# A chain of linear attention and two expert layers: a new order for the first block, and fixed places for five weights of the second expert

## The chip, the cores and the metric

The kernel runs on one core of a Trainium2 chip. The metric is the device time of one execution in microseconds, the median of several runs. PE is the matmul engine (TensorE), DVE the vector engine, ACT the scalar engine, POOL is GpSimd, and SP is the engine whose queue issues nearly all transfers.

## What is computed

```python
def _attn_ref(r, k, v, w, u):            # B, H, S, D = 4, 8, 768, 48
    for t in range(S):
        kt, vt, rt, wt = (k[:, :, t], v[:, :, t], r[:, :, t], w[:, :, t])
        cur = np.einsum('bhd,bhe->bhde', u[None] * kt, vt)
        y[:, :, t] = np.einsum('bhd,bhde->bhe', rt, state + cur)
        state = wt[:, :, :, None] * state + np.einsum('bhd,bhe->bhde', kt, vt)
...
def _moe_ref(x, w1, w2, w3, w_out):      # 3072 tokens, 384 -> 1024 -> 1024 -> 384
    return ((x @ w1) * (x @ w2) @ w3) @ w_out
...
def _moe2_ref(x, w_in, w_out):           # 384 -> 2048 -> 384
    h = x @ w_in
    return (h - np.tanh(h)) @ w_out
```

The weights come as 64-bit floats, the rest as 32-bit floats.

## The kernel before

The 3072 tokens are 24 attention chunks of 128 (chunk 0 to 23) and six blocks of 512 (block 0 to 5); four chunks make the x of one block. Attention works chunk by chunk: DVE runs two scans over the decay (`running`, `backward`), `decayed` multiplies them into r and k, PE makes the scores (`psA`), the transposed keys (`psk`), the state's update (`psu`) and the outputs (`psy`); ACT copies scores out of PSUM, POOL masks them, and DVE or PE puts the term with u on the diagonal (`put_diag`, from chunk 4 on; `diag` before). `x_round` on ACT and `x_rest` on DVE split the result into a rounded value and a remainder, since every large product is made of three products of halves (`three`, lines 206 to 208). Six transfers on SP (`spread`, `xt<-y`) bring the last 16 dimensions of each head into place at the end of a block.

Each block of the first expert has eight parts f: `phase1` makes x·w1 and x·w2 of 128 columns (`psa`, `psb`, 18 products), the gate multiplies them (ACT copies a, DVE multiplies, ACT rounds and DVE takes the remainder of g), and `phase2` adds the part to the block's sums (`acc`, 9 products). w3 and w_out are folded into one matrix W on the chip, in eight folds (`fold`, `psW`, line 486), each of eight products in plain 32-bit.

Weights must be converted before use. `fetch` brings one of 64-bit words into one of three staging buffers (`st`); `scaled` and `tail` on ACT (lines 168 and 174) take its upper part and three more bits; `joined` on DVE (lines 178 and 180) puts them together in one of three buffers (`cm`) or in place; and for the split weights `rounded` on ACT (line 199) and `rest` on DVE or POOL (line 202) make the halves. w1/w2 come in 8 pieces of 768 columns, w_out in 4 of 768, w3 in 16 of 512, and the second expert's weights in 16 of 768 (`w45`).

The order of the work is set in three ways:

- For block 0, the first chunks and all weights of expert one, the list `ORDER` (line 43) names 409 steps one by one. `lwa3` fetches w1/w2 part 3, `waa3`, `wba3`, `wja3` are its scale, tail and join, `wha3` and `wsa3` its halves; `o` stands for w_out, `x` and `y` for the halves of w3. `F0`, `Fa0`, `Fd0` are fold 0 and its halves, `P0` is phase 1 of part 0, `Ga` to `Gs` its gate, `Q0` its phase 2, and `Sa2`, `O2`, `Y2` and the like are attention steps of chunk 2. Each engine gets its instructions in the order of the list.
- Blocks 1 to 4 are written by `pair` (line 779): a pair is one chunk of attention, two blocks ahead, and two parts f of the block, at i = 0 to 3. Its text is the order too.
- Block 5 of expert one (`moe1` with `hooks`) and the six blocks of expert two (`moe2`) are written plainly, and a scheduler orders them; it may put their instructions ahead into places of the pair loop.

Two weights of expert two are converted in the pair loop, in blocks 2 and 3: fetched at i = 1, scaled and joined at i = 2, split at i = 3. The other fourteen are converted by `conv2` from block 5 on. After each block `store` copies the three sums out and takes their largest absolute values, which, with those of the weights (`largest`), decide at the end whether a short series is good enough for the tanh.

Of the kernel before, what the change touches and what calls it, by code (L numbers as in the profile page):

```python
# [15 lines left out]
ALU = mybir.AluOpType  # L16
# [10 lines left out]
KT = DM // 128  # L27
# [13 lines left out]


ORDER = """
LP0 LK0 lwa3 lwa1 lwa2 Da0 LP1 Dr0 K0 Db0 LK1 Dk0 Sd0 Dc0 waa3 wba3 Sa0 Se0 wja3 waa1 Sf0 wba1 St0 lwy3 Sb0 wja1 Sk0
Sm0 SB0 Su0 waa2 SM0 Da1 lwa0 wha3 O0 T0 Dr1 wba2 U0 Db1 LP2 wha1 LK2 V0 Dk1 W0 wsa3 Sd1 X0 Dc1 way3 Se1 wby3 Sf1 Y0
Sa1 wsa1 St1 SB1 Da2 Sb1 SM1 Sk1 wja2 Sm1 waa0 Su1 Dr2 O1 T1 wba0 lwo0 Dk2 U1 Db2 wha2 LP3 Sd2 V1 LK3 wsa2 W1 Se2 Dc2
Sf2 X1 wao0 Y1 Sa2 wja0 St2 Sb2 SB2 Sm2 Da3 lwo1 Sk2 SM2 wbo0 Su2 Dk3 Dr3 wha0 O2 T2 Db3 U2 LP4 wsa0 Sd3 V2 LK4 Dc3
wao1 W2 Se3 X2 wjo0 Sa3 Sf3 SB3 Da4 lwo2 Sb3 St3 SM3 wbo1 Y2 Sm3 Sk3 wjy3 Dr4 O3 Db4 lwo3 wao2 wjo1 Dc4 Su3 LK5 LN4 V3
wbo2 W3 T3 X3 lwa4 wjo2 wao3 U3 Sa4 LP5 wbo3 Y3 lwy0 P0 Sb4 wjo3 SB4 Sm4 Dt4 lwx0 SM4 waa4 De4 St4 LN5 P1 C4 Ga0 Sk4
wba4 Da5 way0 wby0 wja4 Dr5 O4 wax0 Ga1 Dt5 Db5 lwa5 wbx0 Su4 LK6 X4 P2 V4 wha4 T4 Dc5 Gm0 wsa4 Gb0 wjx0 waa5 U4 W4  # L50
lwx2 Sa5 LP6 wjy0 Ga2 wba5 P3 Gm2 lwy2 Sb5 wja5 Gb2 Sm5 SB5 wax2 SM5 Gs2 lwx3 wha5 Y4 wbx2 F0 Da6 Ga3 De5 Dr6 Gm3 LN6
Db6 Gb3 Gs3 Dc6 wsa5 P4 Fa0 Gm1 way2 Fd0 Gb1 Dt6 wjx2 wby2 wax3 Gs1 lwa6 wbx3 wjy2 Sa6 Ga4 P5 wjx3 lwy4 Sb6 SB6 Sm6
De6 lwx1 SM6 Gm4 LN7 waa6 C5 Gb4 F3 wba6 C6 Ga5 Gs4 Dt7 wja6 Gm5 wha6 lwx4 St6 Gs0 F2 Fa3 wsa6 wax1 Sk6 Fd3 wbx1 way4
wjx1 wby4 lwy1 wjy4 Su6 Fa2 O5 wax4 lwx5 Fd2 wbx4 wjx4 Q0 way1 LP7 LK7 V5 X5 T6 lwa7 W5 wby1 U6 Y5 F4 Gb5 wjy1 Gs5
lwx7 LP8 Da7 De7 Dr7 Db7 LN8 F1 Fa4 wax5 Fd4 Dc7 waa7 wbx5 wax7 wjx5 wba7 Da8 lwy6 wbx7 Sa7 Dt8 Fa1 wja7 O6 Sb7 SB7
St7 LK8 V6 Sm7 Fd1 X6 lwy7 Sk7 wjx7 Q1 SM7 way6 Dr8 W6 wha7 lwy5 C7 P6 wby6 wsa7 Y6 wjy6 way7 wby7 Q2 De8 lwx6 Ga6
wjy7 LN9 Su7 Gm6 F7 T7 Gb6 Db8 U7 LP9 Gs6 Dc8 O7 Fa7 way5 Fd7 wax6 Q3 LK9 wby5 X7 wjy5 wbx6 P7 V7 wjx6 W7 Y7 Z7 Q4 Ga7
Gm7 Gb7 F5 Gs7 F6 Fa5 Fd5 Q5 Fa6 Fd6 Q6 Q7
""".split()


# [30 lines left out]
def body(ctx: ExitStack, tc, rT, kT, wP, wS, vN, rN, kN, vT, uB, uN, uP, w12, w3F, wo, w45, out):  # L92
# [466 lines left out]

    def phase3(bp, xt, f, parts):  # L560
# [95 lines left out]
    def largest(f):
        nc.vector.tensor_reduce(
# [87 lines left out]
    with tc.manual_schedule():  # L745
# [17 lines left out]
    def conv2_halves(f):  # L763
        second.pop()
        w45t[f] = halves(early[f], f"w45_{f}", False)
# [10 lines left out]
        preps[n][k] = a1.tile([128, DM], F32, tag=tag, name=k)  # L776
        nc.sync.dma_start(preps[n][k], src[n])

    def pair(blk, i, acc, weights):
        n = (blk + 1) * per + i  # L780
        now = n < NCH
        nx = n + 1 < NCH
        nn = n + 2 < NCH
        out_ = (lambda e: x2d[blk, :, e, :], blk)
        done = lambda f, g: (step(g, lambda: Wt[f], f, NF, acc, out_), drain(LA1))
        f = 2 * i
        if now:
            scores(n)
            scores_out(n, 0)
            mask(n, 0)  # L790
            scores_out(n, 1)
            mask(n, 1)
            turn = n % NC < NC - 1
            if turn:
                turned(n)
                turned_out(n)
        pa, pb = phase1(xtile(blk), f)
        a = gate_a(pa)
        if nn:
# [92 lines left out]

    for blk in range(NB):
        extra = {f: [] for f in range(NF2)}
        if 0 < blk < NB - 1:
            for j in range(6):
                extra[2 * j + 2].append(lambda n=6 * blk - 6 + j: bounds(n))
        if blk == NB - 1:
            extra[2].append(decide)
        if blk == 0:  # L900
            for f in range(NF2):
                extra[f].append(conv2)
        if blk + 1 < NB:
            extra[8].append(lambda: nxt.append(load_x(x2d[blk + 1])))
        moe2(bp, nxt[blk], blk, extra, NF2 - 3 if blk == NB - 1 else NF2)
# [134 lines left out]
```

## Time and profile before

| | us |
|---|---|
| median of 3 runs | 907.2 (905.99 to 907.22) |
| the profiled execution | 908.82 |
| its span, first to last instruction | 907.1 |
| PE busy in the span | 861.9 |
| DVE, ACT, POOL busy | 614.3, 483.0, 227.3 |

The page is to be read stage by stage: block 0 with its weights up to 175 us, the pair loop to about 450, block 5 of expert one to about 510, and then expert two, which goes on to the end. PE takes its instructions strictly in order, so what stands behind a waiting product waits too.

### The profile page before, as it was taken

The numbers are of one execution on the slowest core, as the hardware profiler recorded it, in microseconds if no ns is written. First come the engines' busy times: TensorE is split into PE (matmuls) and PEld (weight loads), VectorE is DVE, ScalarE is ACT, GpSimd is POOL, SyncE is SP. The second block draws the span as 40 slices with busy tenths as digits, with TensorE's granted clock in tenths as the row PEclk, the third lists the DMA queues.
The fourth block names the chain that finished last, engine by engine and source line by source line (L and its number), as shares of the span: only waits on it lengthen the run. The fifth ranks groups of instructions, "written<-read, shape, count | busy, mean of one in ns | idle before, by whom it ended". The sixth has DMA issues, their size and how long they took to land.

```text
span 907.1 us, 12892 instructions
## 1 busy us (share of the span) xinstructions
PE 861.9 (95%) x4762; PEld 690.8 (76%) x4762; DVE 614.3 (68%) x884; ACT 483.0 (53%) x879; POOL 227.3 (25%) x223
## 2 busy tenths in 40 slices
PE   5879999999999999799999899999999999999996
PEld 4766767778777777577888688888888888888885
DVE  6889884365666666665567977667667577586763
ACT  4546652123223224422467766596696786786662
POOL 4356241053344543435226310010010010000000
PEclk9789999999999999899999999999999999999999
DMA  8586574134443364631253020220220310300001
GB/s 287 196 273 201 168 262 129 47 111 129 116 154 109 96 242 134 215 117 53 54 180 134 21 61 1 68 72 0 71 69 1 94 47 1 106 23 0 36 1 38
DMA packets 51623, 93.31 MB, mean 103 GB/s; under 512 B 5152, under 2 KB 22688, under 8 KB 51552
## 3 DMA queue, kind: packets, MB, share of 16 engines
q1 hardware_dynamic: 51552, 92.41, 32.2%
q8 instruction: 39, 0.64, 0.3%
q14 instruction: 32, 0.26, 0.1%
HBM read 80.99 MB, written 9.44 MB: 100 GB/s over the span
## 4 chain that ended last, share of the span: by engine, by line
PE 49%; issue 3%; POOL 2%; DVE 1%; DMA 1%; ACT 1%; SPq 0%; ACTq 0%; POOLq 0%
PE acc L206 8%; PE acc L208 8%; PE acc L207 8%; PE psh L206 7%; PE psh L208 7%; PE psh L207 7%; POOL w L202 1%; DMA st<-w 1%; PE psa L206 1%; PE psa L207 1%; PE psa L208 1%; PE psb L207 1%; PE psb L206 1%; PE psb L208 1%; PE psy L395 0%
## 5 line engine op out<-in xcount | busy, mean ns | idle before, releaser
L516 DVE TENSOR_TENSOR g<-psh,g 128x512 fp32r<-128x512 f32 (+1 forms) x99 | 66.4, 672 | 55.3 <-ACT g L515 55.0
L206 PE MATMUL psh<-xt,w 128*128 128x512 f32 x252 | 98.1, 389 | 0.5 <-DVE g L516 0.5
L208 PE MATMUL psh<-xt,w 128*128 128x512 f32 x252 | 98.0, 389 | 0.0
L207 PE MATMUL psh<-xt,w 128*128 128x512 f32 x252 | 98.0, 389 | 0.0
L206 PE MATMUL acc<-g,w 128*128 128x512 f32 x252 | 98.0, 389 | 0.0
L207 PE MATMUL acc<-g,w 128*128 128x512 f32 x252 | 98.0, 389 | 0.0
L208 PE MATMUL acc<-g,w 128*128 128x512 f32 x252 | 98.0, 389 | 0.0
L515 ACT CAST g<-psh 128x512 fp32r<-128x512 f32 (+1 forms) x99 | 56.3, 570 | 63.0 <-DVE psh L582 63.0
L512 POOL TENSOR_TENSOR xt<-x2l,xt 128x512 fp32r<-128x512 f32 x18 | 24.4, 1366 | 258.4 <-ACT xt L511 258.3
L580 DVE TENSOR_TENSOR psh<-psh,z 128x512 f32<-128x512 f32 (+1 forms) x99 | 67.2, 679 | 27.0 <-ACT z L577 26.7
L581 DVE SCALAR_TENSOR_TENSOR psh<-s,psh 128x512 f32<-128x512 f32 (+1 forms) x99 | 67.1, 678 | 19.0 <-ACT s L578 12.6
L577 ACT ACTIVATE z<-psh 128x512 f32<-128x512 f32 (+1 forms) x99 | 57.6, 582 | 30.9 <-PE psh L208 29.3
L582 DVE SCALAR_TENSOR_TENSOR psh<-s,psh 128x512 f32<-128x512 f32 (+1 forms) x99 | 67.2, 679 | 9.5
L578 ACT ACTIVATE s<-z,qa 128x512 f32<-128x512 f32 (+1 forms) x99 | 70.5, 712 | 2.4
L579 ACT ACTIVATE s<-z,qa 128x512 f32<-128x512 f32 (+1 forms) x99 | 69.0, 697 | 0.0
L515 ACT CAST g<-psb 128x512 fp32r<-128x512 f32 x40 | 23.4, 585 | 84.9 <-DVE psb L843 48.8
L206 PE MATMUL psa<-xt,w 128*128 128x512 f32 x144 | 61.8, 429 | 6.9 <-DMA xt<-y 3.3
L337 POOL TENSOR_SCALAR_AFFINE_SELECT A<-A 128x512 f32<-128x512 f32 x48 | 37.6, 804 | 90.9 <-ACT A L332 90.7
L206 PE MATMUL psb<-xt,w 128*128 128x512 f32 x144 | 56.9, 395 | 2.5 <-ACT a L531 2.2
L208 PE MATMUL acc<-g,W 128*128 128x512 f32 x144 | 56.3, 391 | 2.2 <-DVE W L202 2.2
L206 PE MATMUL acc<-g,W 128*128 128x512 f32 x144 | 57.8, 401 | 0.0
L207 PE MATMUL psa<-xt,w 128*128 128x512 f32 x144 | 57.6, 400 | 0.0
(141 smaller groups left out, 1984.0 us busy)
## 6 DMA issues: line engine op xcount, KB each, us to landing
st<-w SPq DMA_DIRECT2D x24, 768.0 KB, 4.4
st<-w3F SPq DMA_DIRECT2D x16, 512.0 KB, 4.7
P<-wP SPq DMA_DIRECT2D x24, 258.0 KB, 2.8
ws<-wS SPq DMA_DIRECT2D x24, 256.0 KB, 3.4
kd<-kT SPq DMA_DIRECT2D x24, 256.0 KB, 3.8
rd<-rT SPq DMA_DIRECT2D x24, 256.0 KB, 4.0
vn<-vN SPq DMA_DIRECT2D x24, 256.0 KB, 3.6
wb<-wP SPq DMA_DIRECT2D x24, 256.0 KB, 3.4
```

The lines of the kernel that those rows point to most:

```text
L206: nc.tensor.matmul(ps, lhs(0), rhs(1), start=start, stop=False)
L207: nc.tensor.matmul(ps, lhs(0), rhs(0), start=False, stop=False)
L208: nc.tensor.matmul(ps, lhs(1), rhs(0), start=False, stop=stop)
L337: nc.gpsimd.affine_select(out=A, in_=A, pattern=[[0, NP], [1, C]], compare_op=ALU.is_gt, fill=0.0, base=0, channel_multiplier=-1)
L515: nc.scalar.copy(t[:, 0, :], x)
L516: nc.vector.tensor_sub(t[:, 1, :], x, t[:, 0, :].bitcast(F32))
L577: nc.scalar.activation(out=z, in_=p, func=AF.Square)
L578: nc.scalar.activation(out=s1, in_=z, func=AF.Square, scale=QS, bias=qa[:, 0:1])
L579: nc.scalar.activation(out=s2, in_=z, func=AF.Square, scale=QS, bias=qa[:, 1:2])
L580: nc.vector.tensor_mul(p, p, z)
L581: nc.vector.scalar_tensor_tensor(out=p, in0=s1, scalar=QB1, in1=p, op0=ALU.add, op1=ALU.mult)
L582: nc.vector.scalar_tensor_tensor(out=p, in0=s2, scalar=QB2, in1=p, op0=ALU.add, op1=ALU.mult)
```

## The change

`ORDER` is replaced by another list of the same 409 steps, the first line of each is shown here. The rest of the diff:

```diff
 ORDER = """
-LP0 LK0 lwa3 lwa1 lwa2 Da0 LP1 Dr0 K0 Db0 LK1 Dk0 Sd0 Dc0 waa3 wba3 Sa0 Se0 wja3 waa1 Sf0 wba1 St0 lwy3 Sb0 wja1 Sk0
...
+LP0 LK0 lwo0 lwo1 lwx0 Da0 LP1 Dr0 K0 Db0 LK1 Dk0 Sd0 Dc0 wao0 wbo0 Sa0 Se0 wjo0 wao1 Sf0 wbo1 St0 wax0 wjo1 lwy0 Sb0
...
     def store(acc, dst, blk=None):
         for e in range(KT):
-            if blk is not None:
-                nc.vector.tensor_reduce(out=xm[:, e, blk : blk + 1], in_=acc[e], op=ALU.max, axis=AX.X, apply_absolute_value=True)
             o = ev.tile([128, TB], F32, tag="a", name="o")
...
             nc.sync.dma_start(dst(e), o)
+        for e in range(KT if blk is not None else 0):
+            nc.vector.tensor_reduce(out=xm[:, e, blk : blk + 1], in_=acc[e], op=ALU.max, axis=AX.X, apply_absolute_value=True)
...
     second = list(range(NF2))[::-1]
+    early = []
...
         f = second.pop()
-        w45t[f] = halves_of(w45[f], f"w45_{f}", False, not bound)
-        if bound:
-            largest(f)
+        if bound and f < len(early):
+            w45t[f] = halves(early[f], f"w45_{f}", False)
+        else:
+            w45t[f] = halves_of(w45[f], f"w45_{f}", False, not bound)
...
         split_ps(pb, g)
-        if weights and i == 3:
-            conv2_halves(blk - 2)
-            largest(blk - 2)
         if now and turn:
...
-        if weights and i == 1:
+        if i == 0 or (blk, i) == (NB - 2, 1):
             conv2_fetch()
...
         a = gate_a(pa)
+
+        w = blk - 1 if i == 1 else blk if (blk, i) == (NB - 2, 2) else None
+        if w is not None:
+            conv2_act(w)
+        if i == 2 and blk < 3:
+            conv2_halves(blk - 1)
         nc.vector.tensor_mul(pb, pb, a)
         g = gp.tile([128, 2, TB], F32R, tag="g", name="g")
         split_ps(pb, g)
-        if weights and i == 2:
-            conv2_act(blk - 2)
-            conv2_join(blk - 2)
+        if w is not None:
+            conv2_join(w)
         done(f, g)
...
     for blk in range(NB):
         extra = {f: [] for f in range(NF2)}
+        if blk == 1:
+            for f in range(NF2):
+                extra[f].append(lambda f=f: largest(f))
```

So five weights, 0 to 4, are fetched in the pair loop and joined at i = 1 of blocks 1 to 4 and at i = 2 of block 4; weights 0 and 1 are split at i = 2 of blocks 1 and 2, and weights 2 to 4 stay joined until block 5.

Three places of the built order. The first is on PE behind chunk 1, whose last row is the product with `y_148`. Before, chunk 2 follows at once:

```order
L414 MATMUL psy<-y_148 128x128 x3
L327 MATMUL psA<-rd,kd 128x128 x8
L349 MATMUL psk<-ident,kd 128x128 x4
L362 MATMUL psu<-vn,ks 64x48 x8
L389 MATMUL psy<-rd,Sb_117 64x128 x8
L395 MATMUL psy<-A,vn 64x128 x2
L401 MATMUL psy<-ident,vc 64x128 x2
```

and with the change:

```order
L414 MATMUL psy<-y_148 128x128 x3
L486 MATMUL psW<-wo,w_202 128x384 x4
L486 MATMUL psW<-wo,w_254 128x384 x4
L486 MATMUL psW<-wo,w_378 128x384 x4
L486 MATMUL psW<-wo,w_400 128x384 x4
L327 MATMUL psA<-rd,kd 128x128 x8
L486 MATMUL psW<-wo,w_452 128x384 x4
L486 MATMUL psW<-wo,w_444 128x384 x4
```

Folds 0 and 1 (two rows of `psW` each) now stand ahead of chunk 2's scores, and fold 2 behind them.

The second place is on DVE, in block 3, from the product of the gate at the end of the pair i = 2 to the sum that updates the state in i = 3. Before:

```order
L843 TENSOR_TENSOR psb<-psb,a 128x512
L516 TENSOR_TENSOR g<-psb,g 128x512
L178 SCALAR_TENSOR_TENSOR cm<-cm,cl 128x768
L180 SCALAR_TENSOR_TENSOR cm<-st,cm 128x768
L178 SCALAR_TENSOR_TENSOR cm<-cm,cl 128x768
L180 SCALAR_TENSOR_TENSOR cm<-st,cm 128x768
L343 COPY_PREDICATED A<-eye,cd 128x512 x2
L178 SCALAR_TENSOR_TENSOR cm<-cm,cl 128x768
L804 TENSOR_TENSOR psb<-psb,a 128x512
L180 SCALAR_TENSOR_TENSOR cm<-st,cm 128x768
L516 TENSOR_TENSOR g<-psb,g 128x512
L657 TENSOR_REDUCE wm<-w_1_3233 128x3
L370 TENSOR_TENSOR Sb_117<-psu,Sb_118 128x4x48
```

and with the change:

```order
L846 TENSOR_TENSOR psb<-psb,a 128x512
L516 TENSOR_TENSOR g<-psb,g 128x512
L343 COPY_PREDICATED A<-eye,cd 128x512 x2
L804 TENSOR_TENSOR psb<-psb,a 128x512
L516 TENSOR_TENSOR g<-psb,g 128x512
L370 TENSOR_TENSOR Sb_118<-psu,Sb_117 128x4x48
```

The joins of the early weight and of two that had been put ahead from block 5, and the weight's maximum, no longer stand there.

The third place is on POOL in block 2, from the products for the diagonal to the state's decay. Before:

```order
L280 TENSOR_TENSOR rn<-rn,un 128x384
L281 TENSOR_TENSOR rn<-rn,kn 128x384
L337 AFFINE_SELECT A<-A 128x512 x2
L202 TENSOR_TENSOR w_0_2614<-cm,w_0_2614 128x768
L375 TENSOR_TENSOR Sb_117<-Sb_117,P 128x4x48
```

and with the change (weight 1 in place of weight 0):

```order
L280 TENSOR_TENSOR rn<-rn,un 128x384
L281 TENSOR_TENSOR rn<-rn,kn 128x384
L202 TENSOR_TENSOR w_1_2557<-cm,w_1_2557 128x768
L337 AFFINE_SELECT A<-A 128x512 x2
L375 TENSOR_TENSOR Sb_117<-Sb_117,P 128x4x48
```

The subtraction that makes a weight's remainder stands ahead of the masks instead of behind them.

## Rows read from the trace of the kernel before

**Rows 1.** The page's first part: each engine's busy us, share, instructions.

```profile
PE 861.9 (95%) x4762; PEld 690.8 (76%) x4762; DVE 614.3 (68%) x884; ACT 483.0 (53%) x879; POOL 227.3 (25%) x223
```

**Rows 2.** PE's timeline, first block: start us, us, what, count [idle before <-releaser].

```profile
35.44 0.91 PE L414 MATMUL psy<-y 128*128 128x128 f32 x6
...
39.27 0.67 PE L362 MATMUL psu<-vn,ks 128*64 128x48 f32 x16 [1.11 <-ACT ks L354]
...
43.70 0.91 PE L414 MATMUL psy<-y 128*128 128x128 f32 x6
...
60.02 0.50 PE L206 MATMUL psa<-xt,w 128*128 128x512 f32 x1 [1.56 <-DVE xt L434]
...
77.37 1.16 PE L327 MATMUL psA<-rd,kd 48*128 48x128 f32 x16 [1.60 <-POOL kd L303]
...
84.27 5.32 PE L486 MATMUL psW<-wo,w 128*128 128x384 f32 x16
...
130.59 0.50 PE L208 MATMUL acc<-g,W 128*128 128x512 f32 x1 [2.21 <-DVE W L202]
...
175.10 0.39 PE L206 MATMUL psa<-xt,w 128*128 128x512 f32 x1
```

**Rows 3.** DVE's timeline, first block: chunk 2's backward pass begins; chunk 3's last remainder.

```profile
30.39 0.54 DVE L289 RECIPROCAL ends<-R 128x64 f32<-128x64 f32 x1
...
59.41 0.55 DVE L434 TENSOR_TENSOR xt<-psy,xt 128x384 fp32r<-128x384 f32 x1
```

**Rows 4.** Groups by shape, conversions on DVE, ACT: busy us, mean ns | idle.

```profile
L178 DVE SCALAR_TENSOR_TENSOR cm<-cm,cl 128x768 int32<-128x768 int32 x28 | 30.1, 1073 | 12.3 <-ACT cm L168 7.0 <-ACT cd L312 2.9 <-ACT cl L174 2.4
...
L180 DVE SCALAR_TENSOR_TENSOR cm<-st,cm 128x768 int32<-128x768 int32 x24 | 29.9, 1246 | 0.5
...
L180 DVE SCALAR_TENSOR_TENSOR wo<-st,cm 128x768 int32<-128x768 int32 x4 | 5.8, 1454 | 0.1
...
L178 DVE SCALAR_TENSOR_TENSOR cm<-cm,cl 128x512 int32<-128x512 int32 x16 | 12.8, 801 | 6.4 <-ACT cl L174 6.4
...
L180 DVE SCALAR_TENSOR_TENSOR w<-st,cm 128x512 int32<-128x512 int32 x16 | 12.3, 768 | 1.1
...
L202 DVE TENSOR_TENSOR w<-cm,w 128x768 fp32r<-128x768 f32 x8 | 8.7, 1086 | 0.0
...
L168 ACT ACTIVATE cm<-st 128x768 f32<-128x768 f32 x28 | 25.4, 909 | 15.3 <-DMA st<-w 8.4 <-POOL w L202 1.9 <-DVE w L202 1.6
...
L174 ACT ACTIVATE cl<-st,qa 128x768 int32<-128x768 uint8 x28 | 27.9, 996 | 11.5 <-DMA st<-w 9.7 <-DVE cm L178 1.9
```

**Rows 5.** PE's timeline: first rows of blocks 2, 3 and 4, and waits between.

```profile
238.44 0.47 PE L206 MATMUL psa<-xt,w 128*128 128x512 f32 x1
...
308.05 0.47 PE L206 MATMUL psa<-xt,w 128*128 128x512 f32 x1 [1.92 <-ACT A L332]
...
362.75 0.67 PE L362 MATMUL psu<-vn,ks 128*64 128x48 f32 x16 [1.43 <-ACT ks L354]
...
376.56 1.16 PE L327 MATMUL psA<-rd,kd 48*128 48x128 f32 x16 [2.48 <-POOL kd L303]
...
381.63 0.76 PE L206 MATMUL psa<-xt,w 128*128 128x512 f32 x1 [3.33 <-DMA xt<-y]
```

**Rows 6.** Windows, block 4's start: us, PE, PEld, DVE, ACT, POOL, PEclk, DMA.

```profile
380.00:390.00 10.00, 8.37 (x41) 6.57 (x42) 2.93 (x6) 1.51 (x3) 0.00 (x0) 0.72 0.49 140
```

**Rows 7.** DVE's timeline, block 2: the join of an early weight.

```profile
289.77 0.96 DVE L178 SCALAR_TENSOR_TENSOR cm<-cm,cl 128x768 int32<-128x768 int32 x1 [1.08 <-ACT cl L174]
```

**Rows 8.** ACT's and POOL's timelines, block 2's end: remainder's rounding; the masks, twice.

```profile
306.37 0.58 ACT L515 CAST g<-psb 128x512 fp32r<-128x512 f32 x1 [3.46 <-DVE psb L843]
...
290.28 2.25 POOL L337 TENSOR_SCALAR_AFFINE_SELECT A<-A 128x512 f32<-128x512 f32 x2 [4.12 <-ACT A L332]
...
307.51 1.22 POOL L337 TENSOR_SCALAR_AFFINE_SELECT A<-A 128x512 f32<-128x512 f32 x2 [2.37 <-ACT A L332]
```

**Rows 9.** PE's timeline, the last block of expert one.

```profile
504.87 0.61 PE L206 MATMUL psb<-xt,w 128*128 128x512 f32 x1 [2.19 <-ACT a L531]
```

More of the change, by code (lines that the diff above doesn't have):

```diff
@@ L43 @@
 ORDER = """
-LP0 LK0 lwa3 lwa1 lwa2 Da0 LP1 Dr0 K0 Db0 LK1 Dk0 Sd0 Dc0 waa3 wba3 Sa0 Se0 wja3 waa1 Sf0 wba1 St0 lwy3 Sb0 wja1 Sk0
[L45 to L58, printed above, removed]
+LP0 LK0 lwo0 lwo1 lwx0 Da0 LP1 Dr0 K0 Db0 LK1 Dk0 Sd0 Dc0 wao0 wbo0 Sa0 Se0 wjo0 wao1 Sf0 wbo1 St0 wax0 wjo1 lwy0 Sb0
@@ new lines @@
+SB0 Sm0 Sk0 wbx0 SM0 Su0 Da1 lwo2 O0 Dk1 Dr1 T0 way0 Db1 U0 LP2 wby0 wjx0 Sd1 wao2 LK2 V0 Dc1 lwo3 Se1 W0 wbo2 Sf1
+wjy0 X0 Sa1 Sb1 Y0 lwx1 SB1 wjo2 St1 Sm1 Sk1 SM1 Su1 O1 wao3 T1 lwy1 Da2 U1 LP3 wbo3 Dk2 Dr2 wax1 wjo3 Sd2 LK3 V1 wbx1
+W1 way1 X1 Db2 F0 lwy2 wby1 Se2 Sf2 Y1 wjx1 wjy1 lwx2 Fa0 Dc2 F1 lwx3 way2 Fd0 wby2 Dk3 wax2 wjy2 wbx2 wjx2 lwy3 Sa2
+Fa1 Da3 lwx4 wax3 F2 Sb2 Fd1 Dr3 SB2 Sm2 Db3 wbx3 SM2 way3 wjx3 wby3 wjy3 lwy4 St2 wax4 O2 Sk2 Dc3 lwa0 wbx4 Fa2 wjx4
+way4 Su2 LK4 V2 Fd2 lwx5 Sd3 wby4 T2 U2 W2 wjy4 Se3 waa0 Sf3 Sa3 LP4 X2 lwy5 F3 Sb3 Y2 SB3 Sm3 wba0 SM3 wja0 Da4 wha0
@@ new lines @@
+lwa1 St3 Fa3 O3 wsa0 Dr4 Sk3 wax5 Fd3 way5 Db4 wbx5 Su3 LN4 LK5 V3 F4 wby5 T3 Dc4 wjx5 waa1 wjy5 wba1 lwx6 U3 wja1
+lwy6 Dt4 LP5 W3 Fa4 Sa4 X3 Fd4 lwx7 wha1 Y3 F5 De4 wax6 wsa1 LN5 Sb4 SB4 Sm4 wbx6 SM4 Da5 way6 wby6 wjx6 Dr5 St4 Fa5
+Dt5 P0 C4 wax7 lwy7 Sk4 wbx7 wjy6 Fd5 lwa2 wjx7 way7 Su4 Ga0 O4 wby7 T4 lwa3 Gm0 U4 wjy7 Gb0 LP6 F6 V4 LK6 X4 waa2 Gs0
+lwa4 W4 Db5 wba2 waa3 Y4 Dc5 wba3 wja2 P1 Fa6 Fd6 wha2 lwa5 De5 wsa2 LN6 wja3 Sa5 Ga1 waa4 F7 Sb5 Gm1 lwa6 SB5 Sm5 Da6
+Gb1 wha3 SM5 Gs1 wba4 Dr6 wsa3 Dt6 waa5 C5 P2 waa6 wja4 Fa7 wba5 Fd7 wha4 lwa7 De6 O5 wba6 wsa4 LN7 Ga2 Db6 P3 V5 LP7
@@ L59 @@
+LK7 X5 W5 Dc6 Gm2 waa7 Y5 Gb2 wja5 P4 Ga3 Dt7 Gs2 wha5 Gm3 wba7 wsa5 Gb3 Da7 Sa6 Ga4 Gs3 Dr7 Q0 Gm4 Sb6 SB6 De7 Sm6
+Gb4 Db7 LN8 SM6 St6 Q1 Sk6 Gs4 Dc7 C6 Su6 P5 wja6 Dt8 T6 wha6 wja7 U6 O6 LP8 Ga5 Sa7 V6 LK8 wsa6 X6 wha7 Q2 W6 Gm5 Sb7
+Y6 SB7 Sm7 wsa7 Gb5 St7 SM7 Q3 Gs5 Sk7 Da8 Su7 C7 Dr8 P6 T7 Db8 U7 LP9 De8 Dc8 LN9 O7 Ga6 Gm6 Gb6 Q4 LK9 V7 Gs6 X7 W7
+Y7 P7 Z7 Q5 Ga7 Gm7 Gb7 Q6 Gs7 Q7
 """.split()
@@ L750, in body @@
         store(acc0, lambda e: x2d[0, :, e, :], 0)
-    early = []
     def conv2_fetch():
@@ L777, in load_n, with pair @@
         nc.sync.dma_start(preps[n][k], src[n])
-    def pair(blk, i, acc, weights):
+    def pair(blk, i, acc):
         n = (blk + 1) * per + i
@@ L854, in body @@
             for i in range(per):
-                pair(blk, i, acc, blk in (2, 3))
+                pair(blk, i, acc)
     actx.close()
```

## The prediction

> **What bounds the kernel now.** Read the page's busy times first: PE is busy 861.9 of 907.1 us, no other engine over 68% [rows 1]. So the kernel can only get shorter where PE waits or runs slow, and the next view is PE's timeline, read for brackets (idle time ahead of a row) and for rows that take longer than their like. It splits the span into three stretches. Up to 60 us PE does only small attention products: chunk 1's last row starts at 35.44, chunk 2's at 43.70, and the first large product at 60.02 [rows 2]. From there to 175.10, where the loop's first block goes on alone, PE is nearly dense, with two waits, 1.60 and 2.21 us [rows 2]. From 187 to 477 us it is dense but for four waits over 0.25 us, all in or behind blocks 2 and 3 of the pair loop: 1.92, 1.43, 2.48 and 3.33 us [rows 5]. Behind that stand a wait of 2.19 us at 504.87 [rows 9] and the end. The change touches the first and the second stretch.
>
> **The first block.** The same 409 steps stand in another order, so no work is added or taken away; what changes is what PE has while attention is short of data. Before, the eight folds (one takes 5.3 us, [rows 2]) come after chunk 3, ahead of them the w1/w2 conversions. Now six folds stand from behind chunk 1 to ahead of the first product, and the first conversions are w_out and w3.
>
> When can fold 0 start? It needs all four parts of w_out and both halves of w3's part 0 joined on DVE. In the old order DVE had done the same attention steps (through chunk 2's r·k product) at 30.39 [rows 3], together with three joins of 768 columns, 2.32 us each (1.07 + 1.25), and two remainders of 1.09: 9.1 us. The new order has in their place four w_out joins, 2.53 each (1.07 + 1.45), and two w3 joins, 1.57 each: 13.3 us [rows 4]. So DVE is there at about 30.4 + 4.1 = 34.5. On PE, chunk 1's last product ended at 36.35 [rows 2]; its decayed products now stand behind 0.9 us more DVE work (one w_out join and two half joins where a join and a remainder stood). I take 36.35 + 0.9 = **37.2** for the start of fold 0.
>
> What is left on PE from there? From 60.02 to 175.10 the old kernel needed 115.1 us; without its two waits 111.3. To that come chunks 2 and 3, which now run between folds: from one chunk's last row to the next's 43.70 - 35.44 = 8.26, less a wait of 1.11 [rows 2] = 7.15 each, 14.3. So 37.2 + 111.3 + 14.3 = 162.8 if PE never waits. New waits: from below 0, since DVE is ahead. Its work up to chunk 3's last remainder grows by 14.6 us (in come twelve half joins, 18.8, one w_out join, 2.5, and five folds' remainders at half of 1.09, 2.8; out go two w1/w2 joins, 4.6, a half join, 1.6, and three remainders, 3.3), from 59.96 [rows 3] to at most 74.6, and PE reaches the product that needs it at 37.2 + 6 x 5.3 + 14.3 = 83. From above: what PE lost around chunks 2 and 3 in the old order, 60.02 - 36.35 - 14.3 = 9.4. Fold 1 has the least room (its joins come about 5 us behind fold 0's, and fold 0 takes 5.3), so I take 2.5. The block then ends at 165.3 where it ended at 175.1: **-9.8 us** (-12.3 to -2.9).
>
> **The five weights.** Before, the built order holds more than the text of the loop: besides weights 0 and 1, the conversions of weights 2, 3 and 4 had slid forward out of the last block into the end of block 3, three scales and their joins on ACT and DVE at once. There ACT comes late with chunk 19's transposed keys (1.43), POOL then with kd (2.48), and the transfers that fill the next block's xt last (3.33) [rows 5]. At the end of block 2 the rounding of weight 0 stands ahead of the same chain (1.92); the end of block 1, without a weight, has no wait at all (first row of [rows 5]). After the 3.33 us wait PE's granted clock is 0.72 over ten us [rows 6], part of them on the lower of its two levels (1.2 GHz): 2.8 us lost, of which about 0.8 fell into the wait itself, so 2.0. In sum 9.16 + 2.0 = 11.2 us.
>
> Now blocks 1, 2, 3 and 4 hold one conversion each at the second pair and block 4 one more at its third; the order has nothing slid into block 3. What covers them: ACT's two instructions (0.91 and 1.00 us, [rows 4]) stand directly behind the copy of a, where ACT waits 3.46 us for DVE's product anyway [rows 8]. The join on DVE (2.3 us) stands behind the remainder of g, ahead of put_diag; the same place held a join in block 2 of the old kernel [rows 7], and PE did not wait there, since it worked on the next two products. The subtraction on POOL moves ahead of the masks, where POOL waits 4.12 us [rows 8]. If a cover is gone, a place costs up to the 1.43 us of the old block 3. Bounds: 0 to 5 x 1.43 = 7.2; I take 1.1, because four of the five places are like the free one in block 2. **-10.1 us** (-11.2 to -4.0). The fetches (one more in each of blocks 1 and 4 on SP) find one of three staging buffers free, as in block 2.
>
> Beside that join the two masks take 2.25 us on POOL, and 1.22 without one [rows 7, 8]; PE had no wait from it, so it costs nothing. A rule of the Trainium skill speaks against the places all the same: "SBUF — State Buffer", section "Who interferes with whom", has it that a DVE instruction with two SBUF inputs and a GpSimd instruction that reads SBUF shut each other out. The trace agrees with the collision (1.03 us). If all that the rule shuts out came to lie on the path, five joins beside masks would give back 5 x 1.03 = 5.2 us, and the sum would be 892.
>
> **What else is in the diff.** Copies ahead of maxima: the same five DVE instructions in another order; the first sum's bank comes free one DVE instruction later, the stores start earlier, and PE needs the banks only two products on: 0. The maxima of the weights, moved in the text to block 1 of the second expert, stand in the built order close behind each rounding as before, so they move nothing: 0. The last block of expert one has as many conversions left as before (eleven), since the three that slid forward are the ones that now have fixed places: 0, with the wait at 504.87 [rows 9] gone or doubled as bounds, 2.2 us either way.
>
> **Sum.** 907.1 - 9.8 - 10.1 = 887.2 us of span. The profiled execution took 908.82, 1.7 above its span, and the median of the runs is 1.6 below that; so the median comes to **887.3 us**. A measurement here tells about 0.2% (1.8 us) from no change.
>
> **Rivals.**
> - The folds buy nothing: PE is dense between 37 and 83 us but waits afterwards for joins that were put off, and the block still ends at 175. For it: DVE is the busiest engine there, and w1/w2 parts 1 to 7 now follow late. Against: PE's needs come 8 us or more behind DVE. 907.2 - 10.1 = 897 us. Chance 0.12.
> - The fixed places hurt: each of the five costs what the end of block 2 cost, 1.92 us, 9.6 in all, in place of 1.1; 896 us. For it: the masks' collision on POOL, 1.03 us at each place. Against: block 2's join was free. Chance 0.10. (The Trainium skill's rule on the shared port, "SBUF — State Buffer", is one way to it.)
> - Slower: PE takes its queue in order, and fold 0 and 1 stand ahead of chunk 2's scores. If the last part of w_out or a half of w3 lands late (its fetch stands on SP behind chunk 2's loads, which wait for chunk 0's buffers), everything on PE waits, and with it masks, state and the next chunks' loads. Each us of delay is a us of span; it decides from a start of fold 0 at 37.2 + 19.9 = 57 us on. At 60, 910 us. For it: six tiles must be joined by then where three were. Against: twenty us late is twice what PE lost there in all before (9.4). Chance 0.06.
> - The change does less or more than it says: weights 2 to 4 were early already. If fixed places do free the last block after all, the wait at 504.87 and its echo go: 883 us. Chance 0.07.
> - The forecast, 887.3: 0.65.
>
> **How the numbers follow.** The best ends of the three terms, -12.3 - 11.2 - 2.2, give 881.5; the worst, -2.9 - 4.0 + 2.2, give 902.5. 880 to 901 holds the forecast with its bounds, both cases of one gain alone and the case of 883, and leaves out the slower one and the corners. Faster by over 0.2%: 0.90 (all but the slower case, and some room for what no row shows); within: 0.03; slower: 0.07.
>
> **What would show it.** Fold 0 starts on PE at 36 to 39 us, the first product with w1 at 80 to 86, the loop's first block follows at 163 to 168; no PE wait over 1 us at the ends of blocks 2 and 3, and no granted clock under 0.9 there; all other stretches of equal length. The forecast is wrong if PE stands ahead of folds 0 to 2 for more than 5 us, if waits of 1 to 2 us come up at the second pairs of blocks 1 to 4, or if the last block's wait at its end grows.

## The result, and the profile after

The changed kernel takes 882.98 us (median of 4 runs, 882.37 to 886.51) where the kernel before takes 907.21 on the same chip (905.99 to 907.24). The ratio is 0.9735, with a 95% interval of 0.9699 to 0.977: 24.2 us faster. 887.3 was forecast, with a range of 880 to 901.

The page's first lines of the kernel after, to be held against [rows 1]:

```profile
span 881.3 us, 12900 instructions
...
PE   856.6 (97%) x4762; PEld 686.9 (78%) x4762; DVE 616.5 (70%) x884; ACT 485.1 (55%) x879; POOL 227.1 (26%) x223
```

PE has the same 4762 products, and its span is 25.8 us shorter. 20.5 us of that is idle time (907.1 - 861.9 = 45.2 before, 24.7 now). The other 5.3 us is busy time: the same products ran at a higher clock (mean granted clock 0.982 before, 0.991 now).

PE's timeline of the kernel after, first block (start us, us, what, count, idle time before and its releaser), answering to [rows 2]:

```profile
36.63 0.91 PE L414 MATMUL psy<-y 128*128 128x128 f32 x6
37.38 10.49 PE L486 MATMUL psW<-wo,w 128*128 128x384 f32 x32
...
48.89 5.43 PE L486 MATMUL psW<-wo,w 128*128 128x384 f32 x16
...
58.97 0.92 PE L414 MATMUL psy<-y 128*128 128x128 f32 x6
...
82.80 0.48 PE L206 MATMUL psa<-xt,w 128*128 128x512 f32 x1
...
136.49 0.63 PE L349 MATMUL psk<-ident,kd 128*128 128x128 f32 x4 [0.63 <-DVE xt L434]
...
165.45 0.67 PE L362 MATMUL psu<-vn,ks 128*64 128x48 f32 x16
```

Fold 0 starts at 37.38, and folds 0 and 1 run as one row of 32. From there to 136 us no row has a bracket. The last row is the first state update of block 1; in the kernel before it stands at 178.59, so the first block is 13.1 us shorter.

PE's timeline at the starts of blocks 3 and 4, answering to [rows 5], and in the last block of expert one, answering to [rows 9]:

```profile
292.81 0.47 PE L206 MATMUL psa<-xt,w 128*128 128x512 f32 x1
...
359.08 0.47 PE L206 MATMUL psa<-xt,w 128*128 128x512 f32 x1
...
486.82 0.80 PE L206 MATMUL psh<-xt,w 128*128 128x512 f32 x1 [2.13 <-DVE g L516]
```

The waits of 1.92 and 3.33 us are gone, and so are the two inside block 3. Near the end of expert one PE still waits, 2.13 us for 2.19, but it is not the same wait: before, it stood at a product of expert one (`psb`) that waited for ACT's copy of a [rows 9], and now at the first product of expert two's fifth part (`psh`), which waits for DVE's remainder of g and waited 0.54 us before. Around block 4's start the window of ten us (columns as in [rows 6]) has the full clock, 1.00 where 0.72 stood:

```profile
357.00:367.00 10.00, 9.95 (x79) 7.58 (x79) 5.61 (x8) 3.33 (x6) 2.28 (x3) 1.00 0.54 147
```

All kernels of this study can be compared by three marks on PE's timeline: the first product of block 1's fifth part (205.23 before), the first of the last block of expert one (450.92), and the first of expert two's ninth part (529.87). The stretches between them, in us of each profiled execution:

| kernel | to block 1's fifth part | from there to the last block | last block, to expert two's ninth part |
|---|---|---|---|
| before | 205.2 | 245.7 | 79.0 |
| after | 192.1 | 234.4 | 78.3 |
| after, once more (a0) | 193.4 | 234.3 | 76.7 |
| e1, list alone | 192.5 | 246.1 | 79.7 |
| e2, weights and store | 205.9 | 234.2 | 77.2 |
| e3, store alone | 206.6 | 247.4 | 75.9 |
| e5, joins at block ends | 193.3 | 234.7 | 78.3 |
| e6, two places | 194.0 | 238.2 | 77.6 |
| e7, maxima late | 194.3 | 234.2 | 79.6 |
| e8, join three times | 191.4 | 235.4 | 78.4 |
| e10, last block written out | 195.3 | 232.2 | 79.5 |
| e12, halves at block ends | 190.5 | 234.6 | 76.8 |
| e13, folds behind scores | 203.9 | 234.1 | 76.6 |
| e14, start and last block | 192.2 | 232.4 | 85.8 |

From the third mark to the start of PE's last product it is 369.4 us in every row but two (371.1 in e10, 369.5 in e14). The first column lies between 190.5 and 195.3 in the nine rows with the new list as it is (after, a0, e1, e5 to e8, e10 and e12), whose traces show one and the same order of instructions up to the store of block 0; half of this scatter is there at chunk 1's last row already (36.1 to 38.5), since the waits of chunks 0 and 1 differ from execution to execution. In e10 and e14 the second and third columns share an altered border, and only their sum counts.

### The profile page after: what moved, and what is told of

Same layout as the page of the kernel before. It is cut to its first block, busy times and chain, and to the rows that moved or that the text cites. A ratio compares the mean times of both kernels' runs of the same rounds, so it can differ in the third digit from the quotient of the medians.

```text
span 881.3 us, 12900 instructions
## 1 busy us (share of the span) xinstructions
PE 856.6 (97%) x4762; PEld 686.9 (78%) x4762; DVE 616.5 (70%) x884; ACT 485.1 (55%) x879; POOL 227.1 (26%) x223
## 4 chain that ended last, share of the span: by engine, by line
PE 75%; DVE 7%; issue 4%; ACT 2%; POOL 1%; DMA 1%; DVEq 0%; POOLq 0%; ACTq 0%; SPq 0%
PE acc L206 10%; PE acc L207 10%; PE acc L208 10%; PE psh L206 7%; PE psh L207 7%; PE psh L208 7%; PE psa L206 3%; PE psa L208 3%; PE psa L207 3%; PE psb L206 2%; PE psb L207 2%; PE psb L208 2%; PE psA L327 2%; PE psy L395 2%; PE psy L389 2%
## 5 line engine op out<-in xcount | busy, mean ns | idle before, releaser
L516 DVE TENSOR_TENSOR g<-psh,g 128x512 fp32r<-128x512 f32 (+1 forms) x99 | 66.6, 673 | 54.4 <-ACT g L515 53.4
L581 DVE SCALAR_TENSOR_TENSOR psh<-s,psh 128x512 f32<-128x512 f32 (+1 forms) x99 | 67.1, 678 | 19.0 <-ACT s L578 12.3
L206 PE MATMUL psa<-xt,w 128*128 128x512 f32 x144 | 60.6, 421 | 0.1
L206 PE MATMUL acc<-g,W 128*128 128x512 f32 x144 | 58.0, 403 | 0.0
L206 PEld LDWEIGHTS psh<-xt,w 128*128 128x128 f32 x252 | 47.7, 189 | 12.5 <-DVE g L516 2.6
L208 PE MATMUL psa<-xt,w 128*128 128x512 f32 x144 | 56.5, 392 | 0.0
```

The source lines that it names most:

```text
L206: nc.tensor.matmul(ps, lhs(0), rhs(1), start=start, stop=False)
L208: nc.tensor.matmul(ps, lhs(1), rhs(0), start=False, stop=stop)
L516: nc.vector.tensor_sub(t[:, 1, :], x, t[:, 0, :].bitcast(F32))
L581: nc.vector.scalar_tensor_tensor(out=p, in0=s1, scalar=QB1, in1=p, op0=ALU.add, op1=ALU.mult)
```

## The experiments

### The parts alone

e1 is the kernel before with the new `ORDER`. e2 is the changed kernel with the old `ORDER`. e3 is the kernel before with the new `store`:

```diff
         for e in range(KT):
-            if blk is not None:
-                nc.vector.tensor_reduce(out=xm[:, e, blk : blk + 1], in_=acc[e], ...)
             o = ev.tile([128, TB], F32, tag="a", name="o")
...
+        for e in range(KT if blk is not None else 0):
+            nc.vector.tensor_reduce(out=xm[:, e, blk : blk + 1], in_=acc[e], ...)
```

Expected of e1:

> The kernel before with the new list alone. Theory (two separate gains, and the first block's is 13.1 us, as the trace of the changed kernel has it where block 1 begins): 907.2 - 13.1 = 894.1 us, the four waits at the ends of blocks 2 and 3 unchanged (1.9, 1.4, 2.5, 3.3 us). Rival (part of the first block's gain comes with the other edits, or the pair loop gives it back because loads now come earlier): 898 us or more, or other waits in the pair loop.

Measured: 898.77 us beside 909.18, ratio 0.988 (0.985 to 0.9911). That is 10.4 us less, where the theory has 13.1. In the profiled execution, 896.2 us and so 2.6 under the median, the first block's gain is there in full (192.5), and the old waits of the pair loop stand in PE's timeline as before, only earlier:

```profile
296.03 0.47 PE L206 MATMUL psa<-xt,w 128*128 128x512 f32 x1 [1.88 <-ACT A L332]
...
350.71 0.67 PE L362 MATMUL psu<-vn,ks 128*64 128x48 f32 x16 [1.44 <-ACT ks L354]
...
364.45 1.16 PE L327 MATMUL psA<-rd,kd 48*128 48x128 f32 x16 [2.40 <-POOL kd L303]
...
369.29 0.76 PE L206 MATMUL psa<-xt,w 128*128 128x512 f32 x1 [3.09 <-DMA xt<-y]
```

So these waits do not depend on the first block. As the rival has it, some of the gain is given back: a new wait of 0.82 us came up at block 1's end, and the one in the last block is 2.99 us for 2.19.

Expected of e2:

> The changed kernel with the old list. Theory: the pair loop's 11.2 us and the last 0.7 are left: 907.2 - 12 = 895 us; the first block as in the kernel before, no wait over 0.3 us in blocks 2 to 4. Rival (the fixed places cost something that the shorter first block had hidden, or are worth less without it): 898 us or more.

Measured: 893.31 us beside 909.18, ratio 0.9809 (0.9775 to 0.9843), 15.9 us less where the theory has 12. In the profiled execution, 896.38 us and so 3.1 over the median, the first block is as before (205.9), and the pair loop has the changed kernel's length (234.2) without a wait over 0.3 us in blocks 2 to 4. Each of the two gains is there without the other.

Expected of e3:

> The kernel before with the sums copied ahead of their maxima, nothing else. Theory (costs nothing): 906.5 to 907.5 us, the same four waits in blocks 2 and 3. Rival (the sums' banks come free earlier or later at each block's first products): each of the four blocks 1 to 4 moves by up to 0.7 us, 904.4 or 910.0 us.

Measured: 904.99 us, ratio 0.9951 (0.9933 to 0.9969), against a forecast of no change. The profiled execution took 907.66 us, 2.7 over the median. In it the pair loop did not move for the better (247.4, and block 3 has its waits, 3.41 us the longest). The last block did: 75.9 for 79.0. By this profile it isn't the copies of blocks 1 to 4 that pay, but the built order of the last block, which the scheduler makes anew from the text. On DVE, where the sums of block 4 are stored:

```
 L536 TENSOR_TENSOR psb<-psb,a 128x512
-L551 TENSOR_REDUCE xm<-acc 128x1
 L657 TENSOR_REDUCE wm<-w_4_4040 128x3
-L551 TENSOR_REDUCE xm<-acc 128x1
-L516 TENSOR_TENSOR g<-psb,g 128x512
-L551 TENSOR_REDUCE xm<-acc 128x1
-L178 SCALAR_TENSOR_TENSOR cm<-cm,cl 128x768
-L556 COPY o<-acc 128x512
-L180 SCALAR_TENSOR_TENSOR cm<-st,cm 128x768
+L516 TENSOR_TENSOR g<-psb,g 128x512
+L178 SCALAR_TENSOR_TENSOR cm<-cm,cl 128x768
+L554 COPY o<-acc 128x512
+L557 TENSOR_REDUCE xm<-acc 128x1
+L180 SCALAR_TENSOR_TENSOR cm<-st,cm 128x768
+L557 TENSOR_REDUCE xm<-acc 128x1
```

The gate's remainder (L516) now stands ahead of the maxima, and orders further on differ as well. By the table, the nine kernels with the new store and an untouched last block take 75.9 to 78.4 there (mean 77.3), and the two with the old store 79.0 and 79.7: 2.0 us on average. By their traces the nine share one order in the last block on PE, DVE and ACT, and the two share another. Which of the moved instructions pays was not tried, and where the rest of the 4.2 us between the medians (909.18 and 904.99) comes from is not shown.

By their ratios e1 and e2 gain 10.9 and 17.4 us of 909.2, together 28.3, each with some 3 us of uncertainty, where the whole gains 23.1 beside a0's runs of the kernel before. The traces fit better: e1's span is 12.6 us shorter than 907.1, e2's 12.5, and the whole's 25.8. But this is in part luck, since e1's profiled execution lies under its median and e2's over it.

Expected of a0, the changed kernel once more:

> The changed kernel again, beside the next three on one chip: a ratio of 0.9735 to the kernel before, as at first (0.970 to 0.977).

Measured: 886.15 us beside 909.21, ratio 0.9743 (0.972 to 0.9765). As expected.

### The folds: their place on PE

e13 moves folds 0 and 1 in the list behind chunk 2's scores:

```diff
-... Db2 F0 lwy2 wby1 Se2 Sf2 Y1 wjx1 wjy1 lwx2 Fa0 Dc2 F1 lwx3 way2 Fd0 ... lwy3 Sa2 Fa1 ...
+... Db2 lwy2 wby1 Se2 Sf2 Y1 wjx1 wjy1 lwx2 Dc2 lwx3 way2 ... lwy3 Sa2 F0 F1 Fa0 Fd0 Fa1 ...
```

> The changed list with folds 0 and 1 put behind chunk 2's scores. Theory (folds earn by standing ahead of what PE would wait for: chunk 2's decayed keys are ready at 43.2 us, PE is free at 37.4): PE waits 5.8 us there, the first product with w1 comes 5 to 6 us later (88 us for 82.8), and the whole is 5 to 6 us slower than the changed kernel. Rival (DVE bounds the stretch to 83 us, so that the order on PE does not matter): the first product within 1 us of 82.8, the same time.

Measured: 893.41 us, ratio 0.9825 (0.9801 to 0.9849), 7 us slower than a0. Between the profiles the loss is more (a0's execution lies 3.5 us under its median, this one 0.8): the first product with w1 comes at 92.70, 9.0 us behind a0's 83.71, though chunk 1's last row stands at nearly the same time (37.71 and 37.54). PE's timeline, the row of DVE that decays chunk 2's keys, and the windows from the wait to the folds' end:

```profile
44.41 2.08 PE L327 MATMUL psA<-rd,kd 48*128 48x128 f32 x16 [5.79 <-issue]
46.42 17.54 PE L486 MATMUL psW<-wo,w 128*128 128x384 f32 x48
```

```profile
43.62 0.69 DVE L303 TENSOR_TENSOR kd<-kd,ws 128x512 f32<-128x512 f32 x1
```

```profile
38.60:44.40 5.80, 0.02 (x1) 0.02 (x1) 5.16 (x8) 2.60 (x6) 1.25 (x1) 0.61 0.56 200
44.40:50.00 5.60, 5.59 (x22) 3.86 (x23) 1.11 (x2) 1.40 (x3) 0.00 (x0) 0.50 0.33 106
50.00:60.00 10.00, 10.00 (x32) 5.90 (x32) 4.25 (x7) 1.65 (x5) 0.29 (x1) 1.00 0.36 106
```

The wait is the forecast one, 5.79 us. The row names no releaser (`issue`), but the scores read kd, and they start right where DVE's row ends (44.31). Behind the wait the granted clock is 0.50, the lower of its two levels (1.2 GHz), for 5.6 us: chunk 2's scores take 2.08 us for 1.16, and three folds 17.54 where they took 10.49 + 5.43 = 15.92 in the kernel after. So a wait of 5.8 us costs 8.3. The rival, that DVE bounds the stretch, is out: with the same DVE work the first product comes 9 us later.

### The fixed places: what covers them

e8 repeats the second half of the join twice at each place (the result is the same):

```diff
+        for _ in range(2):
+            nc.vector.scalar_tensor_tensor(out=m, in0=st[:, :, 1], scalar=SIGN, in1=m, op0=ALU.bitwise_and, op1=ALU.bitwise_or)
```

> The changed kernel with the second half of each early weight's join done three times, 2 x 1.25 = 2.5 us more of the vector engine at each of the five places (the same values are written again). Theory (the join is covered, by the two products that PE has while DVE is at it, some 6 us a part): no wait of PE over 0.5 us at the places, the same time within 1 us. Rival (the cover is nearly used up: the masks on POOL already take 2.5 us beside the join): up to 5 x 2.5 = 12.5 us more, at least one wait of 1 us at each place.

Measured: 882.84 us, ratio 0.9722 (0.9682 to 0.9762). DVE and POOL at block 2's place:

```profile
259.44 1.27 DVE L180 SCALAR_TENSOR_TENSOR cm<-st,cm 128x768 int32<-128x768 int32 x1
260.74 2.26 DVE L764 SCALAR_TENSOR_TENSOR cm<-st,cm 128x768 int32<-128x768 int32 x2
```

```profile
258.67 2.53 POOL L337 TENSOR_SCALAR_AFFINE_SELECT A<-A 128x512 f32<-128x512 f32 x2 [2.67 <-ACT A L332]
```

PE does not wait at any of the five places. There are waits of 0.61 and 0.48 us at the ends of blocks 1 and 2, and the pair loop is 1.0 us longer (235.4). The five joins are covered with room to spare: 11 us more of DVE work costs about one.

e5 moves scale and join of weights 0 to 2 from the second pair (i = 1) to the fourth, the block's end:

```diff
-        w = blk - 1 if i == 1 else blk if (blk, i) == (NB - 2, 2) else None
+        w = blk - 1 if i == (3 if blk < 4 else 1) else blk if (blk, i) == (NB - 2, 2) else None
...
-        if i == 2 and blk < 3:
-            conv2_halves(blk - 1)
+        if i == 0 and blk in (2, 3):
+            conv2_halves(blk - 2)
```

> The changed kernel with the scales and joins of weights 0, 1 and 2 moved from the second pair of blocks 1 to 3 to the fourth, and the halves of 0 and 1 to the first pair of the next block. Theory (the place decides: at a block's end the transfers into xt stand behind the chain, as at the end of block 2 of the kernel before, 1.92 us): a wait of 1.5 to 3.5 us at the end of blocks 1, 2 and 3, pair loop 5 to 9 us longer than the changed kernel's, 888 to 892 us by the first measurement's scale. Rival (only three conversions at once hurt, a single one is free anywhere): no wait there, within 1 us of the changed kernel.

Measured: 884.33 us, ratio 0.9732 (0.9695 to 0.9769), pair loop 234.7, no wait of PE over 0.25 us at any block's end. My theory falls: a single join is free at the end of a block too.

e6 keeps fixed places for weights 0 and 1 only:

```diff
-        if i == 0 or (blk, i) == (NB - 2, 1):
+        if i == 0 and blk < 3:
...
-        w = blk - 1 if i == 1 else blk if (blk, i) == (NB - 2, 2) else None
+        w = blk - 1 if i == 1 and blk < 3 else None
```

> The changed kernel with fixed places for weights 0 and 1 alone. The built order then lets three conversions slide into the second and third pair of block 2. Theory (what is slid in stands at once on ACT and DVE, and costs as in block 3 of the kernel before, 7.2 us of waits and 1.8 us of slow clock): block 2 is 4 to 9 us longer. Rival (slid conversions are free away from a block's end): block 2 as in the changed kernel, within 1 us.

Measured: 886.41 us, ratio 0.9755 (0.9718 to 0.9792). The pair loop is 238.2 us, 3.8 longer, all of it in blocks 2 and 3. In the built order two conversions slid to the join of weight 1, so that DVE has three joins between 259 and 267 us, and a third slid into the next pair (280 us). PE waits at the block's end. PE's timeline, and the window behind it:

```profile
296.97 0.47 PE L206 MATMUL psa<-xt,w 128*128 128x512 f32 x1 [1.80 <-DMA xt<-y]
```

```profile
296.00:306.00 10.00, 9.03 (x47) 6.85 (x49) 4.53 (x7) 2.38 (x5) 1.80 (x3) 0.83 0.48 133
```

Conversions that the scheduler puts several at a time into a block cost PE a wait at its end and the clock behind it (0.83 over ten us), as in [rows 5, 6], if less here than the 9 us there. I had put the bound at 4; it is just missed.

e12 leaves the joins and moves the halves of weights 0 and 1 to the last place of the block:

```diff
-        if i == 2 and blk < 3:
+        if i == 3 and blk < 3:
             conv2_halves(blk - 1)
```

> The changed kernel with the halves of weights 0 and 1 made in the fourth pair of blocks 1 and 2 instead of the third; the joins stay. Theory (it is the halves, ACT's rounding and POOL's subtraction, that cost 1.92 us at the end of block 2 of the kernel before, not the join, which was free there when tried): a wait of 1 to 2 us at the end of blocks 1 and 2, 2 to 4 us in all. Rival (that wait came from the maximum of the weight or from the load of all of them together): no wait over 0.5 us, the time of the changed kernel.

Measured: 884.15 us, ratio 0.9725 (0.9699 to 0.975), and 0.26 us is the longest wait at these ends. This theory falls too, and the timelines of POOL say a part of why. First the kernel before at the end of block 2, then e12 at the same place:

```profile
295.76 1.81 POOL L202 TENSOR_TENSOR w<-cm,w 128x768 fp32r<-128x768 f32 x1 [3.23 <-ACT w L199]
297.53 1.43 POOL L375 TENSOR_TENSOR Sb<-Sb,P 128x192 f32<-128x192 f32 x1
...
301.79 1.30 POOL L303 TENSOR_TENSOR kd<-kd,ws 128x512 f32<-128x512 f32 x1 [1.16 <-DVE ws L292]
303.05 1.02 POOL L280 TENSOR_TENSOR rn<-rn,un 128x384 f32<-128x384 f32 x1
304.14 1.00 POOL L281 TENSOR_TENSOR rn<-rn,kn 128x384 f32<-128x384 f32 x1
```

```profile
287.41 1.01 POOL L281 TENSOR_TENSOR rn<-rn,kn 128x384 f32<-128x384 f32 x1
288.38 1.83 POOL L202 TENSOR_TENSOR w<-cm,w 128x768 fp32r<-128x768 f32 x1
291.44 1.22 POOL L337 TENSOR_SCALAR_AFFINE_SELECT A<-A 128x512 f32<-128x512 f32 x2 [1.24 <-ACT A L332]
```

Before, the subtraction (1.81 us) stood in the first half of the pair, ahead of the state's decay and of the next chunk's kd and rn. DVE waited 2.17 us for rn (its L285 row at 305.18), the gate's product L843 stood behind that, and ACT's score copy behind the gate; PE's 1.92 us is the end of this chain. In e12 the subtraction stands behind rn, and PE does not wait. Beside the subtraction DVE's scan over the decay (L261) took 2.22 us, where e12's takes 1.22; it ended ahead of the state's decay on POOL, so it was not what the chain waited for.

The subtraction is not the whole cause, since e12 also has the join and the weight's maximum elsewhere. And in e6 block 2 ends in the same way without a subtraction in its last pair:

```profile
293.95 0.55 DVE L285 TENSOR_REDUCE cd<-rn 128x8 f32<-128x384 f32 x1 [2.17 <-POOL rn L281]
...
295.15 0.59 ACT L515 CAST g<-psb 128x512 fp32r<-128x512 f32 x1 [3.47 <-DVE psb L846]
```

DVE's L285 row comes once per pair, so the steps between these rows show where attention falls behind. In block 2 of the changed kernel they are 16.67, 16.72 and 17.03 us. In the kernel before the last one is 18.99 us: 9.99 up to the sum that updates the state (L370), where the join and the maximum stand, and 9.00 behind it, where the subtraction stands; in the changed kernel these are 9.03 and 8.00. In e6 the step over the three joins is 19.18 us, and the next, with the fourth join, 16.65. In e8 the step with the long join is 18.10 us, and the next makes it up with 15.66, though 0.48 us of wait are left at that block's end. So by these rows PE waits at a block's end for a lag of attention that no later pair of the block has made up, and the subtraction is about half of it in the kernel before. This is read from the rows; no run takes out the join, the maximum or the subtraction alone.

### The last block of expert one

The wait of 2.13 us and the slow window behind it (0.83 from 480 to 490 us) were left, so three versions were meant to beat the changed kernel. e7 holds the sixteen maxima of the weights and the last decision on the tanh back:

```diff
-                extra[f].append(lambda f=f: largest(f))
+                extra[f].append(lambda f=f: behind(lambda: largest(f)))
...
+    def behind(x):
+        with tc.issue_after(last[0]):
+            x()
```

> The changed kernel with the sixteen maxima of the weights and the final decision held behind the vector engine's work of the block where the text has them. Theory (in the last block of expert one the vector engine is the bound: between 477 and 487 us it spends 4.0 us on maxima and the check of the weights' tops, ahead of the 2.13 us wait and the slow clock behind it, some 1.7 us): the wait shrinks or goes, 883.0 - 3.8 = 879.2 us at best, 881 as the likeliest. Rival (the wait comes from joins, and what is removed there is only filled by others): 882.5 to 883.5 us. Slower is possible if the late maxima fall on the path of expert two's gate: 884 us.

Measured: 886.34 us, ratio 0.9747 (0.9715 to 0.9778). The wait did not go, but grew and changed its name:

```profile
483.92 0.50 PE L206 MATMUL psb<-xt,w 128*128 128x512 f32 x1 [3.68 <-ACT a L531]
```

The room was filled with other work. On DVE the product of expert one's last gate but one (L536, at 482.06) stands behind five instructions of expert two's gates; ACT's rounding waits for it, the copy of a behind that, and PE for the copy.

e10 writes the last block out: per part one scale and join behind the gate, its halves a part later, kept in that order; one more weight is fetched in block 4.

```diff
-    hooks = {f: [conv2] * (2 if f < 2 else 1) for f in range(NF)}
...
-    moe1(xtile(NB - 1), NB - 1, hooks)
+    with tc.manual_schedule():
+        for f in range(NF):
+            pa, pb = phase1(xtile(NB - 1), f)
+            a = gate_a(pa)
...
+            for _ in range(2 if f == 0 else 1):
+                conv2()
+            if f:
+                conv2_act(w)
```

> The changed kernel with the last block of expert one written out as the pair loop is: one weight's scale and join per part behind the gate's copy and remainder, its halves one part later, the order kept as written. Theory (that block loses 3 to 4 us to its built order: gates of expert one stand behind conversions and behind expert two's first gates): the stretch from the last block's first product to expert two's ninth part, 78.3 us in the changed kernel, gets 3 to 5 us shorter, 878 to 880 us. Rival (DVE has more work than time there, whatever the order): within 1 us of the changed kernel, or longer where a product of expert two waits for a weight.

Measured: 886.45 us, ratio 0.9758 (0.9722 to 0.9795). Last two stretches 232.2 + 79.5 = 311.7 us (after: 312.7), but 1.7 more in the rest. Window 500 to 510 us (us, PE, PEld, DVE, ACT, POOL, clock, DMA):

```profile
500.00:510.00 10.00, 8.42 (x38) 6.64 (x37) 10.00 (x16) 9.02 (x17) 6.80 (x5) 1.00 0.32 96
```

DVE has no idle time there, and not for 30 us: what isn't converted in the last block meets expert two's gates. The rival holds.

e14 takes e10 and e7 together, with two more conversions in the last block (weights 12 and 13), and at the start puts two of ACT's copies ahead:

```diff
+        joins = [[], [5], [6], [7, 8], [9], [10, 11], [12], [13], []]
...
-... Sb0 SB0 Sm0 Sk0 ... wao2 LK2 V0 ...
+... Sb0 Sk0 SB0 Sm0 ... V0 wao2 LK2 ...
```

> A version meant to beat the changed kernel: chunk 0's key copy ahead of the second score copy and chunk 0's output copy ahead of a weight's scale on ACT; the last block of expert one written out with the conversions up to weight 13 in it (one per part, two at parts 3 and 5, where DVE was idle half the time in the run before that wrote it out); the sixteen maxima held back to expert two's second block. Theory: start 1 us shorter (the waits of 2.7 and 1.3 to 2.9 us ahead of chunk 0's state and last output), expert two's start 3 us shorter: 0.969 of the kernel before, 4 us under the changed kernel. Rival (DVE is full for 30 us from expert two's beginning whatever is taken off, as in that run, and the start's waits move to the masks): no gain, or 1 to 3 us slower.

Measured: 889.71 us, ratio 0.9778 (0.9752 to 0.9803). The start came as hoped in size, 81.86 for the first product where the nine kernels with the changed kernel's list have 82.3 to 84.7, but this lies within their scatter. The last two stretches are 5.5 us longer (318.2 for 312.7): five waits of PE between 446 and 484 us, the longest 3.04 us. None of the three beat the changed kernel.

## Why the prediction was right, step by step

**The start of fold 0: right.** 37.2 was forecast, 37.38 came (36.88 to 39.25 in the nine profiles).

**The first block's sum: too small a gain.** -9.8 was forecast (-12.3 to -2.9); it is -13.1 in this profile, and -13.0 by the means of nine kernels with the new list and three with the old, beyond the best end. The product that stood at 175.10 comes at 161.93, ahead of the 163 to 168 named as a sign. The step that failed is "I take 2.5" for new waits: the only one over 0.25 us is 0.63, which makes 1.9 us. The other 1.6 us are in "111.3 + 14.3", which counts the old rows as work: part of them ran at a low clock behind waits. In the kernel before, the window 75 to 85 us has a granted clock of 0.83, in the kernel after 1.00, which is up to 1.7 us. e13 shows the mechanism: put a wait back, and the clock goes with it.

**The pair loop: right, the places cheaper than taken.** -10.1 was forecast, -11.3 came, at the best end of the bounds (-11.2). The waits of [rows 5] and the slow clock of [rows 6] went whole, and the 1.1 us for five places is 0: e8 and e5 show how well they are covered. One cause was named wrongly: at the end of block 2 it is not ACT's rounding that holds the chain up, but POOL's subtraction behind it, and by the rows this gives only about half of the lag that ends in the 1.92 us; the other half stands where the join and the maximum are, and e6 has nearly the same wait (1.80 us) without a subtraction there.

**The collision of the join and the masks** took place as forecast: 2.54 us on POOL in block 2 of the kernel after (at 258.82), 1.23 without a join, and e8 shows that it costs PE nothing. (The Trainium skill, "SBUF — State Buffer", section "Who interferes with whom", has the collision as a rule; the rows agree with it, while the 5.2 us that it would have given back did not come.)

**The store: the step that was wrong.** "Copies ahead of maxima [...] 0" holds for the pair loop, where the order is the text's. In the last block the scheduler orders from the text. e3 alone is faster by 0.31 to 0.67% as a whole, and the table puts a gain into the last block. In the two profiles compared here it shows as 0.7 us; on average over the kernels it is 2.0.

**The last block's wait: right in size, by luck.** The wait of [rows 9] at a product of expert one is gone, and the one of 0.54 us at expert two's fifth part has grown to 2.13. The store alone does this: in e3 the same product waits 2.13 us (at 513.43). The forecast of 0 reasoned with the number of conversions left and did not see that the order would change.

So 882.98 lies 4.3 us under the forecast: 3.3 in the first block, 1.2 in the pair loop, 0.7 in the last block, and 0.7 at the last transfers of the kernel (2.93 us on SP's queue before, 1.69 after), less 1.6 by which the profiled run of before stood above its median.

**The rivals.** "The folds buy nothing" (897) and "the fixed places hurt" (896) are excluded by e1, e2 and e8. The slower case needed a fold 0 at 57 us or later, and it came at 37.38. The fourth case gave the right time, 883, for a wrong reason: it took a freed last block, but a wait of the same size stands there, and the time came from the first block and the pair loop.

## What to carry to other kernels

Work that needs only weights is worth most ahead of the products that the busiest engine would wait for, not behind them: it fills the wait, and it saves the low clock behind it, which e13 puts at 2.5 us for a wait of 5.8. Preparations for a later stage belong one by one at places from which the chain that feeds the next step can make up its lag before the busiest engine needs it; single joins cost nothing here in the second or the fourth pair (e8, e5), while a scheduler that is left to place them puts two or three at once. And an edit that changes no cost by itself can still move the order wherever a scheduler makes it from the text: compare the built order there, not only the diff.

## What was not expected

One and the same list of steps reached block 1's fifth part between 190.5 and 195.3 us in nine profiles, and one and the same order of instructions crossed the last block in 75.9 to 78.4; differences of 2 us between single profiles are not readable in such a kernel. And a join that is made three times over, 11 us more of DVE in all, is hidden almost whole.
